# One square moved from VectorE to GpSimd, one PSUM bank number changed and one crossbar transfer set later on SyncE, in a fused attention and feed-forward kernel

## The chip, the cores and the metric

The kernel runs on one core of a Trainium2 chip. The metric is device time in microseconds (us). A difference of about 0.2%, some 0.7 us here, is what a measurement of this kernel can tell from no change.

The engines are named as in the profile: PE is TensorE (matrix products, with weight loads as PEld), DVE is VectorE, ACT is ScalarE, POOL is GpSimd, SP is SyncE, which issues transfers only.

## What is computed

For 8 batches of 8 heads with 576 rows of 64, a linear attention with a feature map, and a feed-forward network on its output:

```python
def phi(x):
    proj = np.einsum('bhsd,df->bhsf', x, w_phi)
    proj = proj - np.max(np.abs(proj), axis=-1, keepdims=True)
    return np.concatenate([np.exp(proj), np.exp(-proj)], axis=-1)
q_p, k_p = phi(q), phi(k)
kv = np.einsum('bhsf,bhsd->bhfd', k_p, v)
z = np.sum(k_p, axis=2)
num = np.einsum('bhsf,bhfd->bhsd', q_p, kv)
den = np.einsum('bhsf,bhf->bhs', q_p, z)[..., None] + 1e-06
x = (num / den).transpose(0, 2, 1, 3).reshape(4608, 512)
h = np.maximum(x @ w_in, 0.0)          # w_in 512 x 2048
out = h * h @ w_out                    # w_out 2048 x 512
```

All matrix products run in bf16 with sums in f32.

## The kernel before

The 4608 rows of x are worked in nine chunks of 512: chunk c holds the first 512 rows of batch c, and the ninth holds the last 64 rows of all eight batches. While the feed-forward products of chunk c run on PE, the attention of batch c + 1 is worked in between, and the output products of chunk c - 1.

The program is first written down as a list of 1731 steps (`Plan.add`), each with an engine and a function that issues its instructions. The steps are numbered in the order in which they are made; this number is used below ("step 515"). Three tables then fix the schedule:

- `ORDER` lists the steps in the order in which they are issued. `pin` chains each instruction to the one before it on its engine, so each engine, and each engine's transfer queue, works in the order that `ORDER` gives to its own steps. Where steps of two engines stand in `ORDER` relative to each other does not make either wait, apart from the data.
- `BASES` gives the PSUM bank (0 to 7) of each of the 403 uses of PSUM. Some uses take one bank, some two in a row. A new use waits until the last reader of the bank's use before is done.
- `STATES` has one digit for each step that may run on either of two engines: 1 takes the other one.

A fourth table, `GATES`, makes a load on POOL's queue wait for a step of another engine. All loads of q, k, v and the weights are issued on POOL's queue, one behind the other; the crossbar transfers (transposes) and the stores of the output are issued on SP's.

The steps around the change, by their lines:

- First batch (batch 0): step 138, lines 615 to 619, transposes on PE the output of attention (tile xo, 128 rows by 512) into one PSUM bank; steps 139 and 140, line 628, copy the two halves on DVE into the chunk's x tile xT. Steps 152 to 154 and 166 to 168 are the same for the next two groups of rows. The products of the first chunk (line 730, steps 322, 325 and on) take 16 matmuls of 128 columns each, one group of 128 rows at a time; steps 322 and 325 need only the copies 139 and 140.
- Second batch (batch 1): step 215, line 354, projects k for one group of heads: eight matmuls, in turn into the lower and the upper of two banks. Step 216, line 409, takes the maxima on DVE. Steps 221 and 233 are projections of the same kind.
- Step 187, line 549, are two matmuls for the features of q of batch 0. Their exponentials follow on ACT (line 564).
- Second chunk (chunk 1): for each of 16 blocks of 128 of the 2048 hidden columns, four matmuls (line 719), a relu from PSUM into the tile hr (line 694 on ACT, 696 on DVE) and a square from hr into the tile h (line 703, `tensor_tensor` with both inputs hr). hr is a ring of four tiles. Step 514 is the relu of the fifth block, on DVE, step 515 its square, and step 532 the relu, on ACT, that writes the same hr tile again. The squares of the second chunk are read by the output products (line 784) of that chunk, the first reader of step 515 being step 699.
- Crossbar transfers on SP: step 389 (line 338) turns q of batch 2 into qT, step 388 k of batch 2 into kT, and steps 285, 294, 303 and 312 (line 637) turn the four xo tiles of batch 1 into the xT tiles of chunk 1. The first product of chunk 1 waits for all four of these. Step 512 (line 803) is a store of the output.
- On POOL's queue: step 768 and 767 are loads of k of batch 4, steps 573, 575, 576 and 578 are loads of q of batch 3.

The square chooses its engine here:

```python
def engine():
    return nc.gpsimd if now[0].eng == "POOL" else nc.vector
...
pin(engine().tensor_tensor(out=dst, in0=i_, in1=i_, op=ALU.mult))
o = add("DVE", dve_cost(256), fn, r=[("hr", sl)], w=toks, what="sq")
if c < LENT:
    plan.either((o, "POOL", pool_cost(512)))
```

Of the kernel before, what the change touches and what calls it, by code (L numbers as in the profile page):

```python
# [111 lines left out]
def kernel(  # L112
# [833 lines left out]
]  # L946
BASES = (
    '7762205543351613247724322301602306674447442731320126074760270660422244446264622606176160063720462403'
    '6376440226246040224115440556605777123504024764140002202442402462567677750767766755006425602422242222'
    '6400041712301603166777067742404660026444202224400017210165317677737366646061634664004006640006224525'  # L950
    '2454225454357220664133466404400220620232550535444304162615557154625737570741465213753727542242756523'
    '160'
)
STATES = (
    '0000000000000000010100110100110100010010000010000010000000000000100000001000100010100101000000001000'
    '0010000000001010000000100010000101010000100010010001001001111111000110010000001000110100100101000010'
    '011000000101100101001001111100011100100101111010010100010000111111000100001'
)
# [46 lines left out]
```

## Time and profile before

| what | us |
|---|---|
| median of three timed runs | 356.57 (356.17 to 356.60) |
| the profiled execution, whole | 356.65 |
| its span, first to last instruction | 354.6 |
| PE busy | 343.6 |
| DVE busy | 276.7 |
| ACT busy | 227.0 |
| POOL busy | 95.6 |

The profile comes from one execution. Its span is the time from the first to the last instruction; 356.65 - 354.6 = 2.05 us lie around it. Times inside it are given from the start of the span. In a line of the timeline stand the start, the duration (of all instructions of the line together, where xN is more than 1), the engine, the source line, the operation, what it writes and reads, the shapes, and in brackets the idle time before it with what ended it. Matmuls overlap in the pipeline: a line of four matmuls of 512 columns lasts 1.02 to 1.04 us, but the next one starts after 0.86 to 0.87 us. In the same way an instruction of DVE or ACT begins some 0.08 to 0.1 us before the record of the one ahead of it ends.

### The profile page before, as it was taken

Reading aid. Unit: us, or ns where it says so; the run is one execution under the profiler, and the core shown is the slowest. Engines: PE = TensorE matmul, PEld = TensorE weight load, DVE = VectorE, ACT = ScalarE, POOL = GpSimd, SP = SyncE. Lnnn points to the kernel's source line nnn. Section 1 sums busy time; section 2 is a strip of 40 time slices with the busy share of each in tenths; the row PEclk is TensorE's granted clock in tenths of the full one; section 3 lists DMA queues with packets and bytes.
Section 4 is the critical chain, followed back from the end, with each engine's and each line's share of the span. In section 5 each row is a group of like instructions: output and inputs, shape, how many; then the busy total and the mean of one; then the engine's idle time right before and its main releaser. Section 6 shows DMA issues by size and latency. Waiting matters only on the chain.

```text
span 354.6 us, 8429 instructions
## 1 busy us (share of the span) xinstructions
PE 343.6 (97%) x3400; PEld 192.4 (54%) x3400; DVE 276.7 (78%) x525; ACT 227.0 (64%) x428; POOL 95.6 (27%) x143
## 2 busy tenths in 40 slices
PE   7889999999999999999999999999999999999995
PEld 4668976544654555455544644455555544444452
DVE  4998998899979988989778878799889736736210
ACT  4998987599779775795678577769686311340301
POOL 8834450296509500288000820000000000000000
PEclk9999999999999999999999999999999999999999
DMA  8999979999989987899454994700221211010105
GB/s 100 171 197 201 197 89 153 152 117 182 194 160 130 161 140 149 189 98 155 86 115 110 108 200 94 161 9 31 46 46 45 55 38 60 30 59 2 59 1 176
DMA packets 96101, 39.59 MB, mean 112 GB/s; under 512 B 64576, under 2 KB 91584, under 8 KB 96064
## 3 DMA queue, kind: packets, MB, share of 16 engines
q0 software_dynamic: 45216, 18.36, 45.3%
q1 hardware_dynamic: 50528, 20.42, 26.8%
q8 instruction: 26, 0.43, 0.5%
q10 hardware_dynamic: 320, 0.30, 0.3%
q14 instruction: 11, 0.09, 0.1%
HBM read 36.77 MB, written 9.44 MB: 130 GB/s over the span
## 4 chain that ended last, share of the span: by engine, by line
PE 76%; DVE 10%; ACT 7%; DMA 4%; issue 2%; SPq 0%; POOL 0%; DVEq 0%; ACTq 0%; POOLq 0%
PE psum L784 30%; PE psum L719 25%; PE psum L579 5%; PE psum L354 4%; PE psum L730 3%; PE psum L472 3%; DMA xq<-in_q_dram 3%; DVE va L442 3%; PE psum L549 2%; DVE mq L514 2%; DVE h L703 2%; ACT hr L694 1%; ACT kn L415 1%; ACT kp L415 1%; DMA out_dram<-ot 1%
## 5 line engine op out<-in xcount | busy, mean ns | idle before, releaser
L784 PE MATMUL psum<-wout,h 128*128 128x512 bf16 x560 | 133.6, 379 | 0.6 <-DVE ot L195 0.6
L719 PE MATMUL psum<-xT,win 128*128 128x512 bf16 x448 | 106.1, 379 | 0.0
L694 ACT ACTIVATE hr<-psum 128x512 bf16<-128x512 f32 x96 | 55.3, 596 | 46.7 <-PE psum L719 24.5
L784 PEld LDWEIGHTS <-h 128*128 128x128 bf16 x560 | 50.2, 98 | 55.0 <-issue 1.9
L719 PEld LDWEIGHTS <-win 128*128 128x128 bf16 x512 | 47.5, 98 | 53.6 <-issue 3.1
L703 DVE TENSOR_TENSOR h<-hr 128x512 bf16<-128x512 bf16 x144 | 56.3, 415 | 16.4 <-ACT hr L694 15.6
L564 ACT ACTIVATE qp<-psum 128x1024 bf16<-128x1024 f32 (+1 forms) x40 | 37.3, 938 | 23.7 <-PE psum L549 22.1
L514 DVE TENSOR_REDUCE mq<-psum 128x8 f32<-128x1024 f32 (+1 forms) x40 | 44.1, 1109 | 3.7 <-PE psum L354 2.9
L409 DVE TENSOR_REDUCE mk<-psum 128x8 f32<-128x1024 f32 (+1 forms) x35 | 38.1, 1109 | 3.5 <-PE psum L354 3.5
L415 ACT ACTIVATE kp<-psum 128x1024 bf16<-128x1024 f32 (+1 forms) x35 | 32.8, 938 | 10.9 <-DVE mk L409 10.6
L564 ACT ACTIVATE qn<-psum 128x1024 bf16<-128x1024 f32 (+1 forms) x40 | 37.4, 938 | 1.3 <-PE psum L579 1.0
L696 DVE TENSOR_SCALAR hr<-psum 128x512 bf16<-128x512 f32 x48 | 32.6, 685 | 6.7 <-PE psum L719 5.3
L253 POOL DMA_DIRECT2D xv<-in_v_dram x26 | 19.3, 754 | 50.5 <-DVE va L442 47.3
L415 ACT ACTIVATE kn<-psum 128x1024 bf16<-128x1024 f32 (+1 forms) x35 | 32.7, 935 | 0.0
L442 DVE TENSOR_TENSOR va<-xv,va 64x256 bf16<-64x256 bf16 (+2 forms) x68 | 30.4, 461 | 1.6 <-ACT va L434 0.8
L591 DVE TENSOR_TENSOR psum<-psum,en 128x520 f32<-128x520 f32 (+1 forms) x40 | 27.6, 698 | 3.9 <-PE psum L579 2.5
L197 ACT ACTIVATE ot<-psum 128x512 f32<-128x512 f32 x18 | 10.7, 594 | 27.1 <-PE psum L784 27.1
L603 DVE TENSOR_TENSOR xo<-psum,rden 128x512 bf16<-128x512 f32 (+1 forms) x40 | 27.3, 685 | 0.8
L253 POOL DMA_DIRECT2D xk<-in_k_dram x28 | 20.7, 746 | 11.5 <-ACT va L428 6.0
L195 DVE COPY ot<-psum 128x512 f32<-128x512 f32 x17 | 11.5, 684 | 15.1 <-PE psum L784 7.9
L472 PE MATMUL psum<-va,kp 128*128 128x65 bf16 x256 | 19.5, 193 | 0.8 <-DVE va L442 0.4
L273 POOL DMA_DIRECT2D xq<-in_q_dram x24 | 17.5, 733 | 10.3 <-ACT va L428 3.0
(68 smaller groups left out, 404.4 us busy)
## 6 DMA issues: line engine op xcount, KB each, us to landing
out_dram<-ot SPq DMA_DIRECT2D x32, 256.0 KB, 2.7
xk<-in_k_dram POOLq DMA_DIRECT2D x26, 128.0 KB, 4.3
xq<-in_q_dram POOLq DMA_DIRECT2D x24, 128.0 KB, 5.4
xv<-in_v_dram POOLq DMA_DIRECT2D x24, 128.0 KB, 4.3
win<-in_moe_w_in_dram POOLq DMA_DIRECT2D x4, 512.0 KB, 12.1
wout<-in_moe_w_out_dram POOLq DMA_DIRECT2D x4, 512.0 KB, 11.8
xq<-in_q_dram POOLq DMA_DIRECT2D x4, 256.0 KB, 6.1
xv<-in_v_dram POOLq DMA_DIRECT2D x2, 512.0 KB, 9.3
```

Of the source, the lines that this page charges most:

```text
L253: pin(nc.gpsimd.dma_start(out=x[:, a * 512 : z * 512].rearrange("p (h x) -> p h x", x=4 * D), in_=src[b][2 * a : 2 * z, 0:512, :].rearrang ...
L409: pin(nc.vector.tensor_reduce(out=mk_view(g), in_=ps2(pj)[:, :, : n * Fd].rearrange("p e (i f) -> p e i f", f=Fd), axis=AX.X, op=ALU.max, ...
L415: pin(nc.scalar.activation(out=dst[slot][:, :, :n, :].rearrange("p e i f -> p e (i f)"), in_=ps2(pj)[:, :, : n * Fd], func=ACT.Exp, scale= ...
L442: pin(engine().tensor_tensor(out=t[:, :, :D].rearrange("p m (x c) -> p m x c", c=2), in0=x.rearrange("p (m x c) -> p m x c", m=n, c=2), in ...
L472: pin(nc.tensor.matmul(out=o[:, sg, hi, :], lhsT=(kp, kn)[sg][kgroup[pr]][:, j % 2, 2 * hi + j // 2, :], rhs=va[s2][sg][:, 8 * pr + 4 * hi ...
L514: pin(nc.vector.tensor_reduce(out=mqb[:, c, :, :n], in_=ps2(pj)[:, :, : n * Fd].rearrange("p e (i f) -> p e i f", f=Fd), axis=AX.X, op=ALU ...
L564: pin(nc.scalar.activation(out=o, in_=i_, func=ACT.Exp, scale=sgn))
L694: pin(nc.scalar.activation(out=hr[sl], in_=ps1(g), func=ACT.Relu))
L696: pin(nc.vector.tensor_scalar(out=hr[sl], in0=ps1(g), scalar1=0.0, scalar2=None, op0=ALU.max))
L703: pin(engine().tensor_tensor(out=dst, in0=i_, in1=i_, op=ALU.mult))
L719: pin(nc.tensor.matmul(out=o, lhsT=win[mc // 4][:, kc, mc % 4 * P : (mc % 4 + 1) * P], rhs=x, start=(kc == 0), stop=(kc == KC - 1)))
L784: pin(nc.tensor.matmul(out=ps1(g), lhsT=h2[c % 2][mc // 4][:, mc % 4, tt * P : (tt + 1) * P], rhs=wout[mc // 4][:, mc % 4, :], start=(mc = ...
```

## The change

The change is in three tables. In `STATES` one digit turns from 0 to 1 (position 86), which is step 515: the square goes from DVE to POOL. In `BASES` the 28th digit turns from 1 to 2, which is the bank of step 138 (read by steps 139 and 140). `ORDER` is rewritten in a stretch of some 25 lines. Taken by engine, the order of PE, of ACT, and of DVE without step 515, is the same as before. On POOL step 515 stands between the loads 768 and 767. On SP the order 389, 285, 388, 294, 512 becomes 389, 388, 294, 285, 512: the transfer 285 stands behind the transfers 388 and 294. It is still ahead of 303 and 312.

```diff
 ORDER = [
...
-    518, 513, 397, 768, 519, 585, 535, 497, 767, 460, 514, 539, 573, 436, 515, 411, 461, 536, 531, 407, 540, 446,
...
+    518, 513, 397, 768, 519, 585, 535, 497, 460, 514, 539, 536, 436, 515, 411, 461, 407, 531, 767, 540, 446, 402,
...
 BASES = (
-    '7762205543351613247724322301602306674447442731320126074760270660422244446264622606176160063720462403'
+    '7762205543351613247724322302602306674447442731320126074760270660422244446264622606176160063720462403'
...
 STATES = (
-    '0000000000000000010100110100110100010010000010000010000000000000100000001000100010100101000000001000'
+    '0000000000000000010100110100110100010010000010000010000000000000100000001000100010100111000000001000'
```

34 rows, old and new, of the table ORDER are left out of this document.

## The prediction

> **What bounds the kernel now.** I read the page's busy times and its chain first, then the busy time by stages, then the timelines of the places that the change touches.
>
> ```profile
> PE 343.6 (97%) x3400; PEld 192.4 (54%) x3400; DVE 276.7 (78%) x525; ACT 227.0 (64%) x428; POOL 95.6 (27%) x143
> ...
> PE 76%; DVE 10%; ACT 7%; DMA 4%; issue 2%; SPq 0%; POOL 0%; DVEq 0%; ACTq 0%; POOLq 0%
> ```
>
> ```profile
> 30.00:110.00 80.00, 79.31 (x1014) 50.76 (x1010) 73.29 (x136) 64.82 (x121) 35.80 (x54) 1.00 1.16 157
> ```
>
> PE is busy in 97% of the span, and the stages table says the same of the stretch in which the change lies: 79.31 of 80 us for PE, 73.29 for DVE, 64.82 for ACT. PE sets the end. An edit to another engine is worth only the PE idle time that it takes away or makes, and a few such holes are all there is. The change touches two of them.
>
> The first hole is at 29 us. These are PE, DVE and ACT there, from their timelines:
>
> ```profile
> 28.75 0.23 PE L354 MATMUL psum<-wphi,kT 64*128 64x128 bf16 x1
> 29.69 0.38 PE L354 MATMUL psum<-wphi,kT 64*128 64x128 bf16 x7 [0.71 <-DVE xT L628]
> 29.88 0.30 PE L549 MATMUL psum<-qT,wphi 64*128 64x256 bf16 x2
> 30.11 0.40 PE L619 MATMUL psum<-ident,xo 128*128 128x128 bf16 x4
> 30.35 1.06 PE L730 MATMUL psum<-xT,win 128*128 128x128 bf16 x16
> ...
> 33.01 0.40 PE L730 MATMUL psum<-xT,win 128*128 128x128 bf16 x4
> ```
>
> ```profile
> 26.90 0.69 DVE L603 TENSOR_TENSOR xo<-psum,rden 128x512 bf16<-128x512 f32 x1
> ...
> 29.40 0.24 DVE L628 COPY xT<-psum 128x256 bf16<-128x256 bf16 x1
> 29.55 0.68 DVE L603 TENSOR_TENSOR xo<-psum,rden 128x512 bf16<-128x512 f32 x1
> 30.18 1.22 DVE L409 TENSOR_REDUCE mk<-psum 128x8 f32<-128x1024 f32 x1
> 31.32 1.03 DVE L628 COPY xT<-psum 128x256 bf16<-128x256 bf16 x4
> 32.96 1.22 DVE L409 TENSOR_REDUCE mk<-psum 128x8 f32<-128x1024 f32 x1 [0.61 <-PE psum L354]
> ```
>
> ```profile
> 27.52 0.62 ACT L197 ACTIVATE qT<-psum 128x512 bf16<-128x512 bf16 x1
> 27.99 0.63 ACT L197 ACTIVATE kT<-psum 128x512 bf16<-128x512 bf16 x1
> 28.47 0.64 ACT L197 ACTIVATE qT<-psum 128x512 bf16<-128x512 bf16 x1
> 30.22 0.60 ACT L564 ACTIVATE qp<-psum 128x512 bf16<-128x512 f32 x1 [1.10 <-PE psum L549]
> ```
>
> Of the eight matmuls of step 215 the first goes at 28.75, the other seven only at 29.69: the first writes bank 0, the second bank 1, and bank 1 still holds the transposed x of step 138, which the DVE copy (step 140) reads until 29.40 + 0.24 = 29.64. The wait is for a bank, not for data.
>
> The second hole is at 92 us, after the square that is moved (81.34):
>
> ```profile
> 81.34 0.42 DVE L703 TENSOR_TENSOR h<-hr 128x512 bf16<-128x512 bf16 x1
> 81.68 0.68 DVE L696 TENSOR_SCALAR hr<-psum 128x512 bf16<-128x512 f32 x1
> 82.28 1.21 DVE L409 TENSOR_REDUCE mk<-psum 128x8 f32<-128x1024 f32 x1
> 83.53 0.29 DVE L442 TENSOR_TENSOR va<-xv,va 64x256 bf16<-64x256 bf16 x1
> ...
> 91.67 0.41 DVE L195 CAST kv<-psum 128x260 bf16<-128x260 f32 x1
> ```
>
> ```profile
> 90.89 1.02 PE L719 MATMUL psum<-xT,win 128*128 128x512 bf16 x4
> 92.13 0.66 PE L579 MATMUL psum<-kv,qp 128*128 128x65 bf16 x16 [0.21 <-DVE kv L195]
> ```
>
> Here DVE is late: it works from 81.34 on almost without a gap, and PE's L579 at 92.13 starts 0.05 after the copy of kv ends (91.67 + 0.41 = 92.08). Its own turn would have come after four matmuls of 0.216 (30.35 to 33.01 and every L719 line show that dense pace), at 90.89 + 0.86 = 91.75. The hole is 0.38, of which the bracket shows 0.21, because the modelled tail of the last matmul covers the rest.
>
> **The bank (step 138 from bank 1 to 2).** Step 215 then finds bank 1 last used by a transpose that ACT copied out by 27.52 + 0.62 = 28.14, and bank 0 by 28.62. Nothing else holds it: its eight matmuls run at 28.75 and take about as long as the seven did between 29.69 and 29.88, so PE is free near 28.97. Step 187 (L549) follows, some 0.23 long by the distance 29.88 to 30.11: until 29.20. Step 152 (L619) needs bank 3, which ACT releases at 28.47 + 0.64 = 29.11: no wait, until about 29.43. Now the first feed-forward product, step 322 (L730, 30.35), is late next: it reads the copy that ends at 29.64, and PE starts some 0.05 after such an end (29.64 to 29.69 above). So it starts at 29.70 in place of 30.35: **0.65 us**. The rest of the old hole stays, as a wait for data.
>
> Does it hold? The next tight places are steps 233 and 337. DVE has no gap from 29.40 to 32.35 and can't come earlier there, except for some 0.1 in the copies; step 337 needs the last of them, at the latest 32.35 + 0.05 = 32.40, against 33.01 - 0.65 = 32.36. That costs 0.04 at most. DVE's hole of 0.61 before 32.96 closes, ACT's of 1.10 before 30.22 moves forward, so both follow PE. As a bound from below I take 0 (the gain is lost later), from above the 0.71 of the bracket. Step 138 itself must now wait for the use before it of bank 2, whose last reader is DVE's L603 of 26.90; that ends at 27.59, and step 138 had to wait for bank 1 until 28.14 anyway: nothing.
>
> **The square (step 515).** DVE loses one instruction. The next one started 81.68 - 81.34 = **0.34** after it, and that is what DVE gains. Between it and the copy at 91.67 the inputs are there early enough, so DVE comes 0.34 earlier to the copy; PE's start moves from 92.13 to 91.79, still after 91.75. So PE gains 0.34; bounds 0 and 0.38.
>
> On GpSimd no square is in this trace. The nearest row on that engine is the one mask at the start:
>
> ```profile
> 3.73 0.33 POOL L810 TENSOR_SCALAR_AFFINE_SELECT ident<-ident 128x128 bf16<-128x128 bf16 x1
> ```
>
> A square of 512 columns is four times as wide: 1.33 us, if all of 0.33 scales. From below it is DVE's 0.42; from above 2.66, twice the 1.33, because it reads two inputs where the mask reads one. I take 1.33, from the nearest row. (The Trainium skill, GPSIMD Engine Reference, section 3.1 on elementwise work, gives about 2.6 cycles an element for two inputs; that would be an estimate of 1.1 us, and the sum would be the same.)
>
> Its cover is this:
>
> ```profile
> 79.22 0.72 POOL L261 DMA_DIRECT2D xk<-in_k_dram  x1
> ...
> 84.31 1.40 POOL L273 DMA_DIRECT2D xq<-in_q_dram  x2 [2.97 <-ACT va L428]
> ```
>
> ```profile
> 83.05 0.60 ACT L694 ACTIVATE hr<-psum 128x512 bf16<-128x512 f32 x1
> ```
>
> ```profile
> 84.08 1.03 PE L719 MATMUL psum<-xT,win 128*128 128x512 bf16 x4
> ```
>
> POOL is done with step 768 at 79.94, waits for the relu until 81.34, and squares until 82.67. Behind it in the queue are 767 and 573, which now issue from 82.67 to 84.07 (before, they took from 79.94 to 84.31 - 2.97 = 81.34, so 1.40); the next load waited for ACT until 84.31 anyway, so nothing after it is late. 573 brings one part of a q tile whose other parts issue from 84.31 on, and 767 is for the batch after that, so neither is the last to land. The new wait is of another kind: step 532 (ACT, 83.05) overwrites the same hr tile and now waits for GpSimd. It has 83.05 - 82.67 = 0.38 to spare, less some 0.05. The output products that read the square come 7 us later. Nothing is added on PE's path.
>
> **The transfer on SP.**
>
> ```profile
> 59.34 1.26 SPq L637 DMA_TRANSPOSE xT<-xo  x1
> 60.78 3.30 SPq L338 DMA_TRANSPOSE kT<-xk  x1
> ...
> 66.07 2.54 SPq L637 DMA_TRANSPOSE xT<-xo  x2
> ```
>
> The three issues 285, 388, 294 take the same time in another order: 388 issues 1.4 earlier, 294 too, 285 goes from 59.34 to about 64.0. The store and the transfers 303 and 312 behind them (66.07) don't move, and the first product of chunk 1 waits for all four tiles, so for 312. I cost it at **0**; its cover is that 312 is issued 2 us after 285's new place. If a moved transfer were the last to land, the price would be its lateness, at most 4.7.
>
> **The sum.** 0.65 + 0.34 = 0.99. Against the profiled execution: 356.65 - 0.99 = 355.66. It stands 0.08 above the median, so 356.57 - 0.99 = 355.58: I forecast **355.6**, 0.28% faster. What this needs is that later holes don't give it back; from 33 us on they hang on PE, DVE and ACT work that moves along, and on transfers started by that work.
>
> **Rivals.**
>
> *A, the early gain is lost* (the copies or a load with a fixed landing set the time again before 80 us, or the wait at 29.69 isn't for the bank). For it: DVE is nearly full from 30 us on, and DMA is most loaded in that stretch (1.16 in the row of 30 to 110). Against it: the wait ends 0.05 after the copy, and the data of step 215 was there at 28.75, when its first matmul ran. Time 356.57 - 0.34 = 356.2.
>
> *B, DVE's gain doesn't reach PE*, since between 81.7 and 91.7 some input is not there 0.34 earlier. For it: many relus and squares alternate there across ACT and DVE. Against it: DVE has no idle time at its starts. Time 356.57 - 0.65 = 355.9.
>
> *C, GpSimd and DVE hold each other up.* The next DVE instruction with two inputs from SBUF is L442 at 83.53 (with the gain 83.19); the two before it read PSUM. If the square takes 2.2 us, it ends at 83.55; should L442 be held until then, DVE has lost its 0.34 again, and step 532, free at 83.60, ends at 84.20 and gives its bank to the product at 84.08 about 0.17 late: 356.57 - 0.65 + 0.17 = 356.1. This trace has no two such instructions side by side; by the nearest row the square ends at 82.67 and never meets L442. The Trainium skill (SBUF — State Buffer, section "Who interferes with whom") says that a VectorE instruction with two SBUF inputs and a GpSimd one that reads SBUF block each other, whichever starts second. By that rule C holds if the square is long, and not otherwise.
>
> *D, slower: the square on GpSimd takes so long that step 532 is late.* If it takes d, step 532 starts at 81.34 + d + 0.05, ends 0.60 later, and the product at 84.08 waits for that bank: it is late by d - 2.04. The 0.34 is gone too. This eats up the 0.65 at d = 2.69, just at the upper bound of 2.66, and d = 3.5 gives 356.57 - 0.65 + 1.46 = 357.4. For it: no row shows GpSimd at such work, and a first use may cost more. Against it: the mask, also a first use, took 0.33.
>
> **Chances.** Forecast 0.43, A 0.13, B 0.12, C 0.07, D 0.18, other mixtures near 356.6 0.07. A difference of 0.2% (0.71 us: below 355.86 or above 357.28) is about what a measurement of this kernel can tell from no change. The forecast lies only 0.28 beyond that bound: nearly all of its 0.43 and a small part of B make 0.45 faster; D above 357.28 makes 0.15 slower; the rest, 0.40, is within. The range is 355.1 to 357.2: below it is a gain half as large again (0.06), above it the longer half of D (0.13).
>
> **What would show it.** In the new profile: L354 at 28.75 with eight matmuls and no bracket, the first L730 at 29.70, L579 near 91.1 without its bracket, a POOL line L703 of about 1.3 us ending before the ACT relu of step 532, and the xT transfers landing before the first L719 of chunk 1. I am wrong if the first L730 stays at 30.3, if the POOL line is longer than 1.7, or if a later hole grows by what the two places gained.

## The result: 1.20 us faster in the median

| | before | after |
|---|---|---|
| median of twelve runs | 356.52 us | 355.32 us |
| the profiled execution, whole | 356.65 us | 354.84 us |
| its span | 354.6 us | 353.0 us |

The ratio is 0.9968, with an interval from 0.9956 to 0.9980: faster by 0.32%. The forecast was 355.6. The busy times and the chain of the page after, against those of before:

```profile
PE 340.7 (97%) x3367; PEld 192.2 (54%) x3400; DVE 276.1 (78%) x524; ACT 226.8 (64%) x428; POOL 96.6 (27%) x144
...
PE 79%; DVE 8%; ACT 6%; DMA 3%; issue 2%; SPq 0%; POOL 0%; DVEq 0%; ACTq 0%; POOLq 0%
```

One instruction has left DVE (525 to 524), one has come to POOL (143 to 144), and PE is still the bound. That PE shows 3367 matmuls where it had 3400 is no saving: 33 records are missing from this trace (the weight loads are all there), so PE's busy sum can't be compared with the one of before. Starts can be.

The first place, on PE and on DVE after the change:

```profile
27.96 0.40 PE L354 MATMUL psum<-wphi,kT 64*128 64x128 bf16 x8
28.20 0.27 PE L549 MATMUL psum<-qT,wphi 64*128 64x256 bf16 x2
28.41 0.39 PE L619 MATMUL psum<-ident,xo 128*128 128x128 bf16 x4
28.64 1.06 PE L730 MATMUL psum<-xT,win 128*128 128x128 bf16 x16
```

```profile
27.36 0.68 DVE L514 TENSOR_REDUCE mq<-psum 128x4 f32<-128x512 f32 x1
27.96 0.28 DVE L628 COPY xT<-psum 128x256 bf16<-128x256 bf16 x1
28.16 0.20 DVE L599 RECIPROCAL rden<-psum 128x8 f32<-128x8 f32 x1
28.27 0.24 DVE L628 COPY xT<-psum 128x256 bf16<-128x256 bf16 x1
28.43 0.68 DVE L603 TENSOR_TENSOR xo<-psum,rden 128x512 bf16<-128x512 f32 x1
```

The eight matmuls of step 215 run together and the hole is gone, as forecast. What was not forecast is that no hole is left: the first L730 follows its neighbour at once, and doesn't wait for the copy, because the copies come earlier too.

The second place, on POOL and on PE:

```profile
79.69 1.04 POOL L703 TENSOR_TENSOR h<-hr 128x512 bf16<-128x512 bf16 x1 [1.46 <-DVE hr L696]
80.67 0.76 POOL L253 DMA_DIRECT2D xk<-in_k_dram  x1
```

```profile
89.19 1.03 PE L719 MATMUL psum<-xT,win 128*128 128x512 bf16 x4
90.05 0.66 PE L579 MATMUL psum<-kv,qp 128*128 128x65 bf16 x16
```

The square takes 1.04 us on POOL, and L579 starts 0.86 after the four matmuls ahead of it, which is their dense pace: the hole of 0.38 is closed whole. The crossbar transfers on SP:

```profile
57.38 3.06 SPq L338 DMA_TRANSPOSE kT<-xk  x1
60.49 2.59 SPq L637 DMA_TRANSPOSE xT<-xo  x2
63.12 0.60 SPq L803 DMA_DIRECT2D out_dram<-ot  x1
63.77 2.53 SPq L637 DMA_TRANSPOSE xT<-xo  x2
```

kT now comes first and the two xT transfers stand together, in about the time that the three took before (57.38 to 63.08, where it was 59.34 to 65.39).

**Two starts that are not alike.** The spans of the two profiles differ by 1.6, more than the medians. Part of that has nothing to do with the change. PE's first transposes of q wait for a load, in before and in after:

```profile
8.85 0.62 PE L328 MATMUL psum<-ident,xq 128*128 128x128 bf16 x8 [0.96 <-DMA xq<-in_q_dram]
```

```profile
8.10 0.62 PE L328 MATMUL psum<-ident,xq 128*128 128x128 bf16 x8 [0.18 <-DMA xq<-in_q_dram]
```

That load landed 0.75 earlier in the second execution, and the profiles of the experiments lie in between (8.14 to 8.61). So in the table below each start is counted from that of step 138 in the same profile (28.09 before, 27.34 after), just ahead of the first place. The starts of PE are those of its weight loads, of which every trace has all 3400. The table gives, in us, how much earlier than before PE, or at the end ACT, reaches a step:

| step, and its start before | after | bank alone | square alone | transfer alone | bank and square |
|---|---|---|---|---|---|
| 322, first L730 (30.3) | 0.96 | 0.96 | 0.00 | 0.00 | 0.95 |
| 455, L579, past the second place (93.9) | 1.32 | 0.94 | 0.36 | -0.03 | 1.32 |
| 788, L354 (129.1) | 1.39 | 0.93 | 0.43 | -0.03 | 1.39 |
| 1111, L784 (179.0) | 1.26 | 0.90 | 0.41 | -0.09 | 1.20 |
| 840, L354, its second load (181.5) | 0.98 | 0.62 | 0.41 | -0.09 | 0.92 |
| 1700, the last output copy (349.4) | 0.95 | 0.52 | 0.41 | -0.10 | 0.80 |

The bank is worth 0.96 at once, the square 0.43, and near 180 us 0.41 of their 1.39 is given back. The experiments take these apart.

### The profile page after: what moved, and what is told of

Same layout as the page of the kernel before. It is cut to its first block, busy times and chain, and to the rows that moved or that the text cites. A ratio compares the mean times of both kernels' runs of the same rounds, so it can differ in the third digit from the quotient of the medians.

```text
span 353.0 us, 8396 instructions
## 1 busy us (share of the span) xinstructions
PE 340.7 (97%) x3367; PEld 192.2 (54%) x3400; DVE 276.1 (78%) x524; ACT 226.8 (64%) x428; POOL 96.6 (27%) x144
## 4 chain that ended last, share of the span: by engine, by line
PE 79%; DVE 8%; ACT 6%; DMA 3%; issue 2%; SPq 0%; POOL 0%; DVEq 0%; ACTq 0%; POOLq 0%
PE psum L784 30%; PE psum L719 28%; PE psum L579 5%; PE psum L354 4%; PE psum L472 3%; PE psum L730 3%; PE psum L549 2%; DVE va L442 2%; DMA xq<-in_q_dram 1%; DVE mq L514 1%; ACT kp L415 1%; ACT kn L415 1%; DMA out_dram<-ot 1%; DVE mk L388 1%; DVE h L703 1%
## 5 line engine op out<-in xcount | busy, mean ns | idle before, releaser
L784 PE MATMUL psum<-wout,h 128*128 128x512 bf16 x527 | 128.4, 379 | 3.2 <-issue 1.3
L694 ACT ACTIVATE hr<-psum 128x512 bf16<-128x512 f32 x96 | 55.3, 596 | 46.3 <-PE psum L719 24.3
L784 PEld LDWEIGHTS <-h 128*128 128x128 bf16 x560 | 50.2, 98 | 55.2 <-issue 2.0
L564 ACT ACTIVATE qp<-psum 128x1024 bf16<-128x1024 f32 (+1 forms) x40 | 37.4, 940 | 21.9 <-PE psum L549 21.5
L514 DVE TENSOR_REDUCE mq<-psum 128x8 f32<-128x1024 f32 (+1 forms) x40 | 44.1, 1110 | 4.0 <-PE psum L354 3.2
L415 ACT ACTIVATE kp<-psum 128x1024 bf16<-128x1024 f32 (+1 forms) x35 | 32.8, 937 | 11.6 <-DVE mk L409 8.9
L564 ACT ACTIVATE qn<-psum 128x1024 bf16<-128x1024 f32 (+1 forms) x40 | 37.4, 939 | 1.3 <-PE psum L579 1.0
L415 ACT ACTIVATE kn<-psum 128x1024 bf16<-128x1024 f32 (+1 forms) x35 | 32.8, 936 | 0.0
L442 DVE TENSOR_TENSOR va<-xv,va 64x256 bf16<-64x256 bf16 (+2 forms) x68 | 30.4, 462 | 1.6 <-ACT va L434 0.8
L603 DVE TENSOR_TENSOR xo<-psum,rden 128x512 bf16<-128x512 f32 (+1 forms) x40 | 27.3, 686 | 1.0 <-DVE rden L599 0.2
L472 PE MATMUL psum<-va,kn 128*128 128x65 bf16 x256 | 19.6, 193 | 0.0
```

The costliest lines, as they stand in the source:

```text
L415: pin(nc.scalar.activation(out=dst[slot][:, :, :n, :].rearrange("p e i f -> p e (i f)"), in_=ps2(pj)[:, :, : n * Fd], func=ACT.Exp, scale= ...
L442: pin(engine().tensor_tensor(out=t[:, :, :D].rearrange("p m (x c) -> p m x c", c=2), in0=x.rearrange("p (m x c) -> p m x c", m=n, c=2), in ...
L472: pin(nc.tensor.matmul(out=o[:, sg, hi, :], lhsT=(kp, kn)[sg][kgroup[pr]][:, j % 2, 2 * hi + j // 2, :], rhs=va[s2][sg][:, 8 * pr + 4 * hi ...
L514: pin(nc.vector.tensor_reduce(out=mqb[:, c, :, :n], in_=ps2(pj)[:, :, : n * Fd].rearrange("p e (i f) -> p e i f", f=Fd), axis=AX.X, op=ALU ...
L564: pin(nc.scalar.activation(out=o, in_=i_, func=ACT.Exp, scale=sgn))
L694: pin(nc.scalar.activation(out=hr[sl], in_=ps1(g), func=ACT.Relu))
```

## The experiments

Each was timed in five rounds (square_thrice in three) beside the kernel before; the ratios are to that. The kernel before took 356.14 to 356.55 in the different sets, so ratios are compared, not times.

**bank_only.** Only the digit of `BASES`.

```diff
-    '...31613247724322301602...'
+    '...31613247724322302602...'
```

> The kernel before with the bank of step 138 turned from 1 to 2 and nothing else. Theory (two holes of PE, each closed by its own edit): step 215 runs its eight matmuls together, and the first L730 comes 0.65 us earlier against its start of the day, or 0.96 us if the DVE copy of step 139 is also no longer 0.3 us late, as in the profile after the change; the time falls by 0.65 to 1.0 us, to 355.5 to 355.9; the hole at 92 us stays. Rival (the gain of 1.2 us came from the start, where the load of xq landed 0.75 us earlier in that one execution): the time falls by less than 0.3 us.

355.67 against 356.55, ratio 0.9977 (0.9968 to 0.9986): 0.88 faster. PE there:

```profile
28.49 0.40 PE L354 MATMUL psum<-wphi,kT 64*128 64x128 bf16 x8
28.72 0.27 PE L549 MATMUL psum<-qT,wphi 64*128 64x256 bf16 x2
28.93 0.39 PE L619 MATMUL psum<-ident,xo 128*128 128x128 bf16 x4
29.16 1.06 PE L730 MATMUL psum<-xT,win 128*128 128x128 bf16 x16
```

The bank digit alone closes the first hole, and it carries most of the gain.

**square_only.** The digit of `STATES`, with the loads 767 and 573 behind step 515 on POOL.

```diff
-    '...1000100010100101000000001000'
+    '...1000100010100111000000001000'
```

> The kernel before with step 515 on GpSimd between the loads 768 and 767, bank and crossbar transfers as before. Theory: the hole before L579 at 92 us closes, worth 0.34 to 0.40 us, so 356.1 to 356.2; the hole at 29 us stays as in the profile before, and the DVE copy of step 139 starts some 0.3 us after its inputs again, if that wait belongs to bank 1. Rival (DVE's gain is lost on the way to PE): within 0.1 us of the kernel before.

356.15 against 356.55, ratio 0.9996 (0.9975 to 1.0018): by its times no difference can be told. By its profile the hole at 92 us is closed, here too:

```profile
90.66 1.02 PE L719 MATMUL psum<-xT,win 128*128 128x512 bf16 x4
91.52 0.66 PE L579 MATMUL psum<-kv,qp 128*128 128x65 bf16 x16
```

and PE stays 0.41 to 0.43 earlier to the end (the table). That is less than these times can resolve, so the size of the square's part rests on traces.

**transfer_only.** Step 285 behind step 294 in `ORDER`, and nothing else.

```diff
-    389, 285, 388, 294, 512
+    389, 388, 294, 285, 512
```

(SP's steps alone.)

> The kernel before with the crossbar transfer 285 behind 388 and 294 on SyncE and nothing else. Theory: no difference, within 0.15 us of 356.5, since transfer 312 is issued and lands last. Rival: kT of batch 2 lands 1.4 us or more earlier and takes something off PE, so up to 0.3 us faster. The hole at 29 us stays in both.

356.33 against 356.55, ratio 0.9994 (0.9986 to 1.0003): no difference.

**bank_and_square.** Both, with SP's order of before.

```diff
-    '...31613247724322301602...'
+    '...31613247724322302602...'
-    '...1000100010100101000000001000'
+    '...1000100010100111000000001000'
```

> Both the bank and the square, crossbar transfers in the old order. Theory (the two holes add up): the same time as the full change, 355.2 to 355.5. Rival (the transfer's place carries part of the gain, or the holes overlap): 0.3 us or more slower than the full change.

355.19 against 356.55, ratio 0.9961 (0.9949 to 0.9973), the same as the full change within the intervals. The two edits add up, and the transfer carries nothing.

**one_more_dve.** This tests why the bank brought 0.96 and not 0.65. On DVE in the kernel before, the copy of step 139 starts 0.96 after the reduction ahead of it:

```profile
28.11 0.68 DVE L514 TENSOR_REDUCE mq<-psum 128x4 f32<-128x512 f32 x1
29.07 0.29 DVE L628 COPY xT<-psum 128x256 bf16<-128x256 bf16 x1 [0.28 <-PE psum L579]
```

In the kernel after it starts 0.60 after it (27.36 to 27.96). The bracket names L579, but that can't be what the copy needs: in after the copy starts while L579 is still running (27.62 to 28.03). Counted in DVE's stream, semaphore waits included, the copy is the 64th instruction of before, and the one ahead is such a wait. The copy has two semaphores to wait for there, PE's and ACT's; it carries the wait for ACT's itself, and the one for PE's is an instruction of its own. With bank 2 it waits for PE's alone, no separate wait stands ahead of it, and it is the 63rd. If the place makes the copy late, one more instruction ahead of it must help. Here the memset of ident at the start (step 3) is issued twice in the kernel before.

```diff
         now[0] = op
         op.fn()
+        if op.seq == 3:
+            op.fn()
```

> The kernel before with the short memset of ident on DVE issued twice at the start (0.1 us in idle time), so that every later instruction of DVE stands one place further on; bank, square and transfer as before. In all profiles so far an instruction of DVE or ACT in a place that is a multiple of 64 on its engine (semaphore waits counted) sometimes starts 0.21 to 0.25 us late when the instruction ahead of it is a semaphore wait. Theory (the late DVE copy at 29.07 comes from its place 64, not from bank 1): the copy starts without the 0.28 hole, the wait of L354 shrinks from 0.71 to about 0.4 us, and the time falls by about 0.3 us. Rival (the copy is late since bank 1 was read by ACT just before): the hole of 0.28 stays, no difference in time.

355.88 against 356.32, ratio 0.9986 (0.9977 to 0.9995): faster by doing one thing more. DVE and PE:

```profile
27.91 0.68 DVE L514 TENSOR_REDUCE mq<-psum 128x4 f32<-128x512 f32 x1
28.51 0.28 DVE L628 COPY xT<-psum 128x256 bf16<-128x256 bf16 x1
```

```profile
28.55 0.23 PE L354 MATMUL psum<-wphi,kT 64*128 64x128 bf16 x1
29.11 0.38 PE L354 MATMUL psum<-wphi,kT 64*128 64x128 bf16 x7 [0.34 <-DVE xT L628]
```

The copy, now the 65th and still behind its separate wait, follows the reduction after 0.60, without a gap (in square_only and transfer_only it is the 64th and starts after 0.96, like before). PE still waits for the bank, but 0.34 where it was 0.71. Counted as in the table, this kernel is 0.38 ahead of before at step 322 and 0.41 at the end. So the late copy, by 0.36, was a cost of its own in before, and the bank digit removed two things: the late start, by chance, for 0.38 of its 0.96, and the wait for the bank for the other 0.58.

**one_more_act.** The reverse side. Near 180 us the kernel after loses 0.28 that before did not. These are DVE, ACT and PE after:

```profile
176.22 1.21 DVE L409 TENSOR_REDUCE mk<-psum 128x8 f32<-128x1024 f32 x1
```

```profile
177.80 1.02 ACT L415 ACTIVATE kp<-psum 128x1024 bf16<-128x1024 f32 x1 [2.47 <-DVE rden L599]
```

```profile
179.27 0.38 PE L549 MATMUL psum<-qT,wphi 64*128 64x512 bf16 x2
179.79 0.29 PE L354 MATMUL psum<-wphi,qT 64*128 64x128 bf16 x4
```

and these DVE and ACT before:

```profile
178.23 1.22 DVE L409 TENSOR_REDUCE mk<-psum 128x8 f32<-128x1024 f32 x1
```

```profile
179.54 1.02 ACT L415 ACTIVATE kp<-psum 128x1024 bf16<-128x1024 f32 x1 [2.06 <-DVE mk L409]
```

The exponential kp starts 1.31 after the start of the maxima mk in before. In after kp starts 1.58 after mk: 0.27 late. The L354 behind it starts 0.52 after L549 (0.24 in before, 181.29 to 181.53). In ACT's stream a relu of the first chunk (L694) has one semaphore wait more with bank 2, which makes kp ACT's 320th instruction, five times 64, right behind a wait; in before it is the 319th. Here the exponential of step 1004, ahead of it, is issued twice.

```diff
         op.fn()
+        if op.seq == 1004:
+            op.fn()
```

> The changed kernel with one small ACT instruction (step 1004, 0.21 us, in front of 2.3 us of idle time at 173 us, writing the same values again) issued twice. Theory (the late kp of ACT at 177.80 comes from its place 320): it starts 0.25 us sooner after the maxima, PE's L354 near 179.8 follows without its hole of 0.14, and the time is about 0.27 us below the changed kernel, 355.0 to 355.1. Rival (the lateness belongs to what it waits for): the hole stays, 355.3.

354.85 against 356.32, ratio 0.9958 (0.9946 to 0.9971): 1.47 faster than before, where after is 1.20. The intervals overlap, so the times don't show that it is faster than after. What the trace shows is the stall itself:

```profile
179.59 0.38 PE L549 MATMUL psum<-qT,wphi 64*128 64x512 bf16 x2
179.84 0.29 PE L354 MATMUL psum<-wphi,qT 64*128 64x128 bf16 x4
```

The L354 is again 0.25 behind L549, and kp, at place 321, 1.31 after mk (176.54 to 177.85): the late start has gone with the place. The added exponential cost nothing there, since ACT had been idle. That this gain reaches the end is not shown. Counted as in the table, this profile is 1.11 ahead of before at steps 1111 and 840 alike, so it loses nothing between them. But it loses 0.44 near 212 us, where an output copy waits 0.48 for a store and PE for the copy, and it ends 0.67 ahead of before, where after ends 0.95 ahead.

**square_thrice.** The square of step 515 issued three times on POOL, for the rivals C and D.

```diff
-                pin(engine().tensor_tensor(out=dst, in0=i_, in1=i_, op=ALU.mult))
+                for _ in range(3 if now[0].eng == "POOL" else 1):
+                    pin(engine().tensor_tensor(out=dst, in0=i_, in1=i_, op=ALU.mult))
```

> The changed kernel with the GpSimd square issued three times (the same result each time): 3.1 us in place of 1.04, to 82.8. Theory of the prediction (rival D there): the relu of step 532 on ACT starts 1.4 us later, the product that takes its bank is about 1.1 us late, DVE's gain is gone, and the time is 1.0 to 1.5 us above the changed kernel, 356.3 to 356.8. Rival C: DVE's L442 at 81.36, with two inputs from SBUF, can't start or end until GpSimd is done at 82.8, and the square after it is late as well; without it L442 starts at 81.36 and takes 0.29 as before. Rival (step 532 has more room than I count): within 0.3 us of the changed kernel.

356.68 against 356.32, ratio 1.0012 (1.0003 to 1.0021): slower than before. POOL, DVE, ACT and PE (lines behind the edit are one higher):

```profile
79.83 3.27 POOL L704 TENSOR_TENSOR h<-hr 128x512 bf16<-128x512 bf16 x3 [1.47 <-DVE hr L696]
```

```profile
80.26 1.21 DVE L409 TENSOR_REDUCE mk<-psum 128x8 f32<-128x1024 f32 x1
81.50 0.63 DVE L442 TENSOR_TENSOR va<-xv,va 64x256 bf16<-64x256 bf16 x1
82.14 1.24 DVE L704 TENSOR_TENSOR h<-hr 128x512 bf16<-128x512 bf16 x1
83.31 0.68 DVE L514 TENSOR_REDUCE mq<-psum 128x4 f32<-128x512 f32 x1
```

```profile
83.13 0.60 ACT L694 ACTIVATE hr<-psum 128x512 bf16<-128x512 f32 x1 [1.53 <-POOL h L704]
```

```profile
81.66 1.02 PE L720 MATMUL psum<-xT,win 128*128 128x512 bf16 x4
83.78 3.89 PE L720 MATMUL psum<-xT,win 128*128 128x512 bf16 x16 [1.10 <-ACT hr L694]
```

Both rivals are real mechanisms, and both need a longer square. D: the relu of step 532 waits for POOL, and PE waits 1.10 for the relu; the prediction's d - 2.04 gives 1.23 for 3.27, and counted as in the table PE loses 1.26 there. C: the two DVE instructions with two inputs from SBUF take 0.63 and 1.24 beside the squares, where the same ones took 0.29 and 0.42; the reduction mk from PSUM keeps its 1.21. L442 begins during the second square, which ends at 81.98, and ends at 82.13; L704 begins during the third, which ends at 83.10, and ends at 83.38. So each was done only after the square that it met. The Trainium skill (SBUF — State Buffer, section "Who interferes with whom") says that one of such a pair blocks the other, and the trace agrees. In the kernel after, the square is over at 80.73, before the first of them starts at 81.36:

```profile
80.11 1.21 DVE L409 TENSOR_REDUCE mk<-psum 128x8 f32<-128x1024 f32 x1
81.36 0.29 DVE L442 TENSOR_TENSOR va<-xv,va 64x256 bf16<-64x256 bf16 x1
81.66 0.42 DVE L703 TENSOR_TENSOR h<-hr 128x512 bf16<-128x512 bf16 x1
```

**ot4, ot_spare, spare_and_act.** These look at the other hole near 176 us, before output products. PE waits there for an output copy (step 1138), and that copy for a store, so that its tile comes free:

```profile
176.35 2.75 PE L784 MATMUL psum<-wout,h 128*128 128x512 bf16 x12 [0.70 <-DVE ot L195]
```

```profile
175.61 0.69 DVE L195 COPY ot<-psum 128x512 f32<-128x512 f32 x1 [2.11 <-DMA out_dram<-ot]
```

The ring got a fourth tile: a new one (ot4), the idle tile otl (ot_spare), and that with step 1004 twice (spare_and_act).

```diff
+    ot.append(otl)
...
-            sl = oslot[0] % 3
+            sl = oslot[0] % 4
```

> The changed kernel with four output tiles ot in place of three. Theory: the hole of 0.70 before L784 at 176.35 (DVE's copy into ot waits for a store that lands at 175.52) closes, and 0.5 to 0.7 us go off, to 354.6 to 354.8, as one fewer wait on DVE also moves the places that are multiples of 64 there. Rival (the transfers of x on SyncE are late in that stretch anyway, and the next product waits for them): less than 0.2 us.

> The changed kernel, with the otherwise idle tile otl (the last chunk's) as a fourth output tile in the ring of three. If the hole of 0.70 before the output products near 176 us comes from the wait for an output tile that the store of step 960 still reads, its bracket goes and PE is up to 0.7 earlier there; what of that reaches the end is 0 to 0.7, so 354.6 to 355.3. If the stores only land late for want of bandwidth, the wait comes back at the next tile and the time stays at 355.3.

> The changed kernel with the fourth output tile and with step 1004 issued twice on ACT, which moves the exponential kp off ACT's place 320. If the two holes near 176 and 180 us are separate, both brackets are gone and the time is some 0.4 below the fourth tile alone: 354.2 to 354.9. If they stand in for one another, it is that of the better of the two, 354.9 to 355.3.

355.36 (ratio 0.9969, 0.9958 to 0.9981), 355.30 (0.9970, 0.9958 to 0.9982) and 355.47 (0.9979, 0.9969 to 0.9989): no faster than after (0.9968). But these kernels don't do the same work. `ORDER` was written for three tiles: with four, the copy 941 and the store 745, and the copy 1138 and the store 942, share a tile while the later copy is issued ahead of the earlier store, so those two stores send a later tile's rows, and wait for them. Part of the output isn't the reference's, and the time holds waits that a right kernel wouldn't have. These three decide nothing.

**one_spare, one_spare_act.** The same idea done rightly: only the copy of step 1138 and its store use otl. The second one also has step 1004 twice.

```diff
             sl = oslot[0] % 3
             oslot[0] += 1
+            o_t = otl if len(plan.ops) == 1138 else ot[sl]
...
-                copy(ot[sl], ps1(g))
+                copy(o_t, ps1(g))
```

> The changed kernel, in which the one output copy that closes late near 176 us (step 1138, with its store 1139) uses the otherwise idle tile otl, and every other copy keeps its tile of the ring of three. The hole of 0.70 before the output products at 176.35 should go, since nothing that is still being stored has to be waited for; the stall of 0.25 at 178 stays. Where the end depends on that hole it comes 0.5 to 0.7 earlier, at 354.6 to 354.9; where another wait stands behind it (a load or a transfer with its own landing), it stays at 355.2 to 355.4.

> The same with step 1004 issued twice on ACT, which moves the exponential kp off ACT's place 320. If both holes are paid for at the end, the time is 0.7 to 1.1 below the changed kernel, 354.2 to 354.6; if a later wait takes back what they gave, 354.9 to 355.3 like the doubled step alone.

354.56 and 354.50 against 356.32, ratios 0.9955 (0.9942 to 0.9967) and 0.9946 (0.9932 to 0.9959). PE in one_spare:

```profile
175.06 3.62 PE L784 MATMUL psum<-wout,h 128*128 128x512 bf16 x16
178.60 0.40 PE L354 MATMUL psum<-wphi,kT 64*128 64x128 bf16 x8
178.84 0.38 PE L549 MATMUL psum<-qT,wphi 64*128 64x512 bf16 x2
179.19 0.29 PE L354 MATMUL psum<-wphi,qT 64*128 64x128 bf16 x4
```

The hole is gone, and counted as in the table one_spare is 1.41 ahead of before at step 788, about as after is, but 2.13 at step 1111, 2.02 at step 840 and 2.01 at the end, where after has 0.95. So in this profile what came free at 176 us reaches the end. kp, again in place 320, is late here too (1.59 after mk, 175.61 to 177.20), but 0.6 earlier than in after, so part of that is hidden: L354 is 0.35 behind L549, not 0.52. That leaves little for the doubled step to win, and it adds 0.06 on top, less than can be told. These two have the lowest medians of the study, 1.76 and 1.82 below before; their intervals just overlap that of after.

## Why the prediction was right

The forecast was 355.6 with a range from 355.1 to 357.2; the median is 355.32. The mechanism held at both places. The sum of 0.99 agrees with the trace's 0.95 at the end, but two of its terms were too small and one loss was missing.

- *What bounds the kernel*: right. PE set the end, and both edits were worth the PE holes that they closed.
- *The bank, 0.65*: mis-sized, it was **0.96**. The step that failed is "the first feed-forward product, step 322, is late next: it reads the copy that ends at 29.64". That took the copy as fixed. It was 0.36 late in before, and this went with the bank, so the copy ended too early to matter (29.64 - 0.36 + 0.05 = 29.33) and PE's own turn, which the prediction put near 29.43, became the limit: 30.35 - 29.43 = 0.92. Of the 0.96, 0.38 is the late start (one_more_dve). The bracket of 0.71 was not the bound from above that it was taken for: the next term of the chain was late for a reason that the same edit removed. A row of before showed DVE idle for 0.28 just there, and the prediction did not ask why.
- *The square, 0.34*: it was **0.36** past the place and **0.43** at step 788. L579 lost all of its hole of 0.38. The remaining 0.07 comes in at the next L579, that of step 455: it starts 0.43 after the L549 ahead of it in before (93.58 to 94.01) and 0.36 in after (91.50 to 91.86). What it waited for is open.
- *The square's time on POOL, 1.33 with bounds from 0.42 to 2.66*: measured 1.04. Scaling the mask by its width was 0.29 too much. The estimate of 1.1 from the figure of the Trainium skill (GPSIMD Engine Reference, section 3.1) was nearer, and the trace agrees with it. The slack of step 532 was 0.38 by the forecast; the square ends at 80.73 and the relu starts at 81.35, 0.62 later, and no wait for POOL appeared.
- *The transfer, 0*: right, shown alone (0.9994, 0.9986 to 1.0003) and by its absence (bank_and_square).
- *"Later holes don't give it back"*: wrong by 0.41. Of that 0.28 (1.26 to 0.98 in the table) is kp's late start on ACT's 320th place, a consequence of the bank digit (bank_only loses 0.28 there, square_only nothing). The rest is the hole at 176 us, which grew by 0.14, from 0.56 to 0.70: the copy, held by its store, came 2.01 earlier (177.62 to 175.61), PE had come 2.15 earlier. Why the store did not come as much earlier is open. Rival A named this kind of loss, but for the stretch before 80 us.
- *Rivals*: A and B did not occur where they were placed: the bank's gain is still 0.94 at 94 us, and the square's reaches PE. C and D did not occur at 1.04, and square_thrice shows that they would with a square of 3.27.

Two terms were too small by 0.31 and 0.09, and a loss of 0.41 was missing: that the sum came out was partly luck. The timed 1.20 (0.7 to 1.6 by the interval of the ratio) can't tell it from 0.95.

## What to carry to other kernels

A bracket prices a hole only up to the next thing that is late, and that thing may itself start late for a reason which the same edit touches: before costing "the copy ends at such a time", see whether the copy started when its inputs were there. A changed bank or engine also adds or removes semaphore waits, and can move far-off instructions by a few tenths of a us. Where a short wait for a buffer stands on the critical engine, give the one late user a spare buffer and leave the rest of the order alone.

## What the runs showed of the hardware

**A late start at some 64th places.** At some places in the streams of DVE and ACT that are a multiple of 64, semaphore waits counted, an instruction right behind a semaphore wait started later than the same instruction at another place. Measured from the start of what stands ahead of it (for kp, of the maxima that it needs):

| instruction | at the 64th place | at another place |
|---|---|---|
| copy (L628) on DVE | 0.96 at 64 (before, square_only, transfer_only) | 0.60 at 65 (one_more_dve) |
| kp (L415) on ACT | 1.58 to 1.59 at 320 (after, bank_only, bank_and_square, one_spare) | 1.31 at 319 (before) and 321 (one_more_act, one_spare_act) |
| xo (L603) on DVE near 199 us | 0.43 to 0.45 at 448 (after, bank_only, bank_and_square) | 0.24 at 449 (before) and 447 (one_spare) |
| qp (L564) on ACT near 256 us | 1.61 to 1.62 at 448 (before, square_only, transfer_only, one_more_dve) | 1.33 at 449 (after, bank_only) |

That is 0.2 to 0.36 us of lateness. Moving the instruction by one place removed it, and moving another one there brought it. Not every multiple shows it: where the engine was still busy with the work ahead, nothing was seen, and the reduction of L514 at DVE's place 256 (before, 112.19) starts 0.04 after its wait, as it does at place 254 (after), though DVE was idle ahead of it. So neither the full condition nor what in the engine is the cause was shown.

**GpSimd and VectorE.** A square of 128 x 512 in bf16 takes 1.04 us on GpSimd against 0.42 on VectorE; three in a row take 3.27. Beside them two VectorE instructions with two inputs from SBUF took 2.2 and 3 times as long (0.63 for 0.29, 1.24 for 0.42), and a reduction from PSUM took its usual 1.21.
